# Partial sums of the second product added in DRAM by accumulating transfers, in a two-layer kernel with linear attention ahead of it

## The chip, the cores and the metric

The kernel runs on one core of a Trainium2 chip. A core has a matrix engine (TensorE, PE in the profile, with its weight loads counted apart as PEld), a vector engine (VectorE, DVE), an engine for functions of one operand (ScalarE, ACT), a general one (GpSimd, POOL) and one that here only issues transfers (SyncE, SP). SBUF is the working memory, PSUM holds the sums of the matrix products in banks, and DRAM holds inputs, outputs and buffers. Each engine works through its own list of instructions in order. The metric is the device time of one execution, in microseconds (us); lower is better.

## The reference

Eight batches and eight heads of 576 rows of 64 values are first taken through linear attention and a normalisation; the heads are then laid side by side, so that 4608 tokens of 512 values go through two dense layers with a softplus between them.

```python
kv = einsum('bhsd,bhse->bhde', k, v)
out = einsum('bhsd,bhde->bhse', q, kv)
x = out / sqrt(mean(out * out, -1) + 1e-6) * g_norm   # (8, 8, 576, 64)
x = x.transpose(0, 2, 1, 3).reshape(4608, 512)
h = x @ w_in                                          # w_in  (512, 2048)
g = maximum(h, 0) + log1p(exp(-abs(h)))
result = g @ w_out                                    # w_out (2048, 512)
```

The last line is the second product. The result has 4608 x 512 values of 32 bits.

## The kernel before, in words

**Tiles and phases.** The 4608 tokens are 36 tiles of 128 rows (t), and 12 blocks of three tiles, 384 tokens (n). The 2048 middle columns are 16 chunks of 128 (c). A step is one block with one chunk: the first product gives 128 x 384 values of h in a PSUM bank (mm1, L660, twelve matrix instructions, since each factor is split into three parts that TensorE multiplies and adds up); ScalarE applies the softplus (L683) and rounds off a first part (L685); VectorE makes the second and third part (L672, L676); and the second product adds the chunk's share to three banks of 128 x 512 sums, one for each tile of the block (mm2, L667, nine instructions).

The split weights of 16 chunks don't fit, so the work is cut into three phases (ENDS, L184): in phase 0 the first four blocks take chunks 0 to 3 and the others 0 to 5, in phase 1 chunks 4 to 7 and 6 to 10, in the last phase the rest. That is 64, 56 and 72 steps, in the order phase, block, chunk (ORDER, L243). Phase 0 also does the attention: it builds kv, multiplies by q, normalises (rows, with the root taken on POOL in L528 and L529) and stores the x of later blocks in DRAM. In the other phases x is loaded again (x_again, L638) and split again (L445 on ScalarE, L448 and L452 on VectorE).

**Partial sums between phases.** At the end of a block in a phase the three banks hold partial sums. `leave` (L708) has ScalarE evict each into an SBUF buffer (L711), and SP stores it (L726) in a buffer in DRAM of its own, one for each phase and tile. When the block comes round in the next phase, `enter` (L701) has SP load that buffer (L704) and ScalarE copy it into the bank (L706), and the second product goes on adding to it: its first instruction starts a new sum only in phase 0 (L668). In the last phase the eviction multiplies by a factor (scale, from whole_scale, 1 + 1/4096 unless a weight is out of range) and the store goes to the output.

**Turned tiles.** For tiles 12 to 32 the rows of x were transposed in blocks of 32 x 32 by VectorE, which leaves the tokens of a block in another order. Their results go to the output in four stores of 32 rows each (L718 to L721) instead of one.

**What sets the order.** The program is written in a fixed order by a planner (Plan, L41). Each piece of work is a task with an engine, a cost in ns, the tasks it follows, a position, and the buffers it takes and gives back; a transfer also has a cost for the DMA engines. The planner plays these through and emits each engine's instructions in the order it found. What a task really waits for at run time is set by semaphores. SBUF buffers of 128 x 512 values come from a ring of 13 (m), two more from a ring called x; the second product's banks are the rings s0, s1 and s2, with one bank each, so a block's bank must be evicted before the next block's sums can begin.

```python
def mm2(i):
    if c == cs[0] and ph == 0:
        new(mine[i], [P, d_model])
    for m in range(3):
        nc.tensor.matmul(mine[i].tile, lhsT=gv.tile[:, m, i * P:(i + 1) * P], rhs=w_out.tile[:, m],
                         start=(ph == 0 and c == cs[0] and m == 0), stop=(c == cs[-1] and m == 2),
                         skip_group_check=True)
```

The functions in full, with the line numbers of the profile:

Of the kernel before, what the change touches and what calls it, by code (L numbers as in the profile page):

```python
# [8 lines left out]
F32 = mybir.dt.float32  # L9
# [3 lines left out]
AF = mybir.ActivationFunctionType  # L13
ALU = mybir.AluOpType
# [4 lines left out]
P = 128  # L19
# [4 lines left out]
E = 1.0 / RADIX  # L24
# [16 lines left out]
class Plan:  # L41
# [15 lines left out]
    def slot(self, ring):  # L57
        return Slot(ring)

    def add(self, engine, ns, run, after=(), pos=0.0, take=(), give=(), size=0, behind=None, follows=None):  # L60
        t = Task(engine, ns, run, [a for a in after if a is not None], pos, list(take), list(give), size)
        for s in t.give:
            s.readers += 1
        self.tasks.append(t)
        t.follows = follows
        t.behind = behind
        return t
# [79 lines left out]
def kernel(  # L147
# [24 lines left out]
    nc = tc.nc  # L172
    B, H, S, D = q.shape
    d_model, d_ff = moe_w_in.shape
# [5 lines left out]
    TB = NT // P  # L180
    n_blocks = n_tokens // NT
    n_tiles = n_tokens // P
# [5 lines left out]
    LAST = PHASES[-1]  # L188
# [4 lines left out]
    CONVERT, FETCH, EARLY, LATER = P0[:8], P0[8:16], P0[16:27], P0[27:]  # L193
    BY_PE = 12
# [7 lines left out]
    dram = ctx.enter_context(tc.tile_pool(name="dram", bufs=1, space=DRAM))  # L202
# [10 lines left out]
    scale = const.tile([P, 1], F32, name="scale")  # L213
# [9 lines left out]
    slot, add = plan.slot, plan.add  # L223

    def new(s, shape, dtype=F32):
        if s.ring == "o":
            s.tile = o_banks[:, :, s.place]
            return s.tile
        pool = ps if s.ring in PS else sb
        s.tile = pool.tile(shape, dtype, tag=f"{s.ring}_{s.place}", name=f"{s.ring}_{s.place}")  # L230
        return s.tile
# [21 lines left out]
    factors_done = {}  # L253
# [156 lines left out]
    BL = 32  # L410
# [232 lines left out]
    part = {}  # L643
# [3 lines left out]
    def step(s):  # L647
        ph, n, c = ORDER[s]
        cs = CHUNKS[ph, n]
        h, g, gv = slot("h"), slot("g"), slot("gv")  # L650
        if c == cs[0]:
            sums[:] = [slot(f"s{i}") for i in range(TB)]
        xv, w_in, w_out = xv_slots[ph, n], w_slots[0, c], w_slots[1, c]
        mine = list(sums)

        def mm1():
            hp = new(h, [P, NT])
            for m in range(3 * KD):
                i, kd = divmod(m, KD)
                nc.tensor.matmul(hp, lhsT=w_in.tile[:, i, kd * P:(kd + 1) * P], rhs=xv.tile[:, i, kd],  # L660
                                 start=(m == 0), stop=(m == 3 * KD - 1))

        def mm2(i):
            if c == cs[0] and ph == 0:
                new(mine[i], [P, d_model])
            for m in range(3):
                nc.tensor.matmul(mine[i].tile, lhsT=gv.tile[:, m, i * P:(i + 1) * P], rhs=w_out.tile[:, m],  # L667
                                 start=(ph == 0 and c == cs[0] and m == 0), stop=(c == cs[-1] and m == 2),  # L668
                                 skip_group_check=True)

        def low():
            nc.vector.tensor_tensor(out=gv.tile[:, 1], in0=g.tile, in1=gv.tile.bitcast(F32)[:, 0], op=ALU.subtract)  # L672

        def less():
            f32 = gv.tile.bitcast(F32)
            nc.vector.scalar_tensor_tensor(out=gv.tile[:, 2], in0=f32[:, 1], scalar=-RADIX, in1=f32[:, 0],  # L676
                                           op0=ALU.mult, op1=ALU.add)

        a = mm1s[s] = add("PE", 2100, mm1, x_split[ph, n] + factors_done[0, c] + [mm1s.get(s - 1)] +

                (factors_done[1, ORDER[s - 2][2]] if s > 1 else []), s, [h],
                ([xv] if c == cs[-1] else []) + ([w_in] if s == last_step[c] else []))
        a = add("ACT", 490, lambda: nc.scalar.activation(new(g, [P, NT]), h.tile, func=AF.Softplus, scale=1.0 + E),  # L683
                [a], s, [g], [h])
        a = add("ACT", 530, lambda: nc.scalar.activation(new(gv, [P, 3, NT], F32R)[:, 0], g.tile, func=AF.Copy, scale=DOWN),  # L685
                [a], s, [gv])
        a = add("DVE", 570, low, [a], s, [], [g])
        a = add("DVE", 570, less, [a], s)
        for i in range(TB):
            last = c == cs[-1]  # L690
            seed = [enter(ph, n * TB + i, mine[i], s + 1)] if ph and c == cs[0] else []
            a2 = add("PE", 700, lambda i=i: mm2(i), [a] + factors_done[1, c] + [mm2s.get(i)] + seed, s + 1.5,
                     [mine[i]] if c == cs[0] and not ph else [],
                     [gv] + ([w_out] if s == last_step[c] else []))
            mm2s[i] = a2
            if last:
                leave(ph, n * TB + i, mine[i], a2, s + 1.5)

    sums, mm2s = [], {}

    def enter(ph, t, bank, pos):  # L701

        pt = slot("m")
        ld = add("SP", 350, lambda: nc.sync.dma_start(out=new(pt, [P, d_model]), in_=part[ph - 1, t][0]),  # L704
                 [part[ph - 1, t][1]], pos - EARLY[10], [pt], [], 900, behind=int(pos) - 4)
        return add("ACT", 600, lambda: nc.scalar.copy(new(bank, [P, d_model]), pt.tile), [ld], pos, [bank], [pt])  # L706

    def leave(ph, t, bank, done, pos):  # L708

        ot = slot("m" if ph == 0 else ("m", "x", "m")[t % TB] if ph == LAST else "m")  # L710
        a = add("ACT", 690 if ph == LAST else 600, lambda: nc.scalar.activation(  # L711
            new(ot, [P, d_model]), bank.tile, func=AF.Copy, scale=scale if ph == LAST else 1.0),
            [done] + (scale_done if ph == LAST else []), pos, [ot], [bank])
        if ph == LAST and BY_PE <= t < n_tiles - TB:
            n, i = divmod(t, TB)

            def store():
                for m in range(P // BL):  # L718
                    a, u = divmod(P // BL * i + m, TB)
                    row = n * NT + u * P + a * BL  # L720
                    nc.sync.dma_start(out=out[row:row + BL], in_=ot.tile[m * BL:(m + 1) * BL])  # L721

            part[ph, t] = None, add("SP", 1600, store, [a], pos, [], [ot], 750)
            return
        dst = out[t * P:(t + 1) * P] if ph == LAST else dram.tile([P, d_model], F32, name=f"part{ph}_{t}")
        st = add("SP", 350, lambda: nc.sync.dma_start(out=dst, in_=ot.tile), [a], pos, [], [ot], 720)  # L726
        part[ph, t] = dst, st

    def whole_scale(pos):

# [25 lines left out]
    for c in range(KF):  # L756
        for j in (2 * c, 2 * c + 1):
            pos = CONVERT[j] if c < 4 else LATER[c - 4] + LATER[12] * (j % 2)
# [11 lines left out]
    for s in range(len(ORDER)):  # L770
        if s == first_step[LAST, 0]:
            whole_scale(s - 4)
        step(s)
# [42 lines left out]
```

## Time and profile before

| | |
|---|---|
| median of nine runs | 908.25 us (907.71 to 911.38) |
| the profiled execution, own time | 909.17 us |
| its span, first instruction to last | 907.4 us |
| mean granted clock of TensorE | 0.996 |
| PE busy | 894.7 us |
| ACT busy | 482.7 us |
| of it, copies of partial sums into banks (L706) | 39.2 us, 72 of them |
| POOL busy | 82.7 us |
| transfers: stores of partial sums, loads of them | 72 and 72, of 256 KB |

The profile shows one execution. A row of a group gives line, engine, operation, what it writes and reads, shapes and count, then busy time in us and the mean length of one in ns, and then how long the engine was idle just before, with the line that ended the wait. A row of a transfer gives how many there were, their size, and the median time from the issue to the landing of the data. "SPq" is the list of transfers that SP issues. A share of busy time is a mean over the whole span; phases 1 and 2, in which the partial sums are loaded and copied, run from about 367 us on.

### The profile page before, as it was taken

The page shows a single profiled execution, that of the slowest core. Times are in us where ns is not written, and L with a number is a line of the kernel's source. Part 1 is how long each engine was busy: PE and PEld are TensorE (multiplying, and loading weights), DVE is VectorE, ACT ScalarE, POOL GpSimd, SP SyncE. Part 2 cuts the span into 40 slices and gives each one's busy share as a digit, 9 for nine tenths or more (in the row PEclk, how much of TensorE's full clock was granted, in tenths as well). Part 3 has the DMA queues.
Part 4 walks back from the last instruction along what each step waited for, and adds up shares of the span by engine and source line. Part 5 has one row for each costly group of instructions (what it writes and reads, how often), then busy time and mean ns, then how long its engine had stood idle before and what let it go on. Part 6 is the DMA issues. An engine that isn't in the chain of part 4 may idle for free.

```text
span 907.4 us, 15751 instructions
## 1 busy us (share of the span) xinstructions
PE 894.7 (99%) x5984; PEld 789.5 (87%) x5984; DVE 577.0 (64%) x982; ACT 482.7 (53%) x932; POOL 82.7 (9%) x79
## 2 busy tenths in 40 slices
PE   7999999999999999999999999999999999999998
PEld 5677888888888899999899998989999998999987
DVE  6887888676577877867666667786424444444442
ACT  4776555433444556765656666665433444444453
POOL 0433322122213200000000000000000000000000
PEclk8999999999999999999999999999999999999999
DMA  9999978578672626366344346551330433333322
GB/s 251 258 207 284 248 173 227 133 164 184 185 156 47 164 94 186 105 199 184 105 128 129 128 152 204 186 167 35 105 105 1 140 105 103 107 105 104 105 70 71
DMA packets 211837, 131.60 MB, mean 145 GB/s; under 512 B 102704, under 2 KB 185648, under 8 KB 211760
## 3 DMA queue, kind: packets, MB, share of 16 engines
q1 hardware_dynamic: 211600, 130.59, 52.7%
q8 instruction: 47, 0.77, 0.4%
q14 instruction: 30, 0.25, 0.1%
q10 hardware_dynamic: 160, 0.00, 0.0%
HBM read 91.75 MB, written 38.80 MB: 144 GB/s over the span
## 4 chain that ended last, share of the span: by engine, by line
PE 95%; DMA 3%; ACT 1%; SPq 0%; DVE 0%; issue 0%
PE h L660 44%; PE s L667 44%; DMA m<-in_v_dram 2%; PE o_banks L521 2%; PE tp L502 2%; PE h L780 1%; PE s L502 1%; DMA m<-x 0%; PE tp L577 0%; DVE xv L448 0%; PE tp L539 0%; ACT m L599 0%; ACT xv L445 0%; PE h L374 0%; ACT x L590 0%
## 5 line engine op out<-in xcount | busy, mean ns | idle before, releaser
L660 PE MATMUL h<-xv,w 128*128 128x384 f32 x2304 | 433.8, 337 | 0.2 <-ACT w L378 0.2
L667 PE MATMUL s<-w,gv 128*128 128x512 f32 x1728 | 432.7, 395 | 0.0
L660 PEld LDWEIGHTS h<-xv,w 128*128 128x128 f32 x2304 | 406.3, 188 | 15.7 <-ACT w L378 0.7
L667 PEld LDWEIGHTS s<-w,gv 128*128 128x128 f32 x1728 | 319.7, 188 | 61.3 <-DVE gv L676 0.2
L672 DVE TENSOR_TENSOR gv<-g,gv 128x384 fp32r<-128x384 f32 x192 | 106.6, 555 | 260.3 <-ACT gv L685 259.8
L683 ACT ACTIVATE g<-h 128x384 f32<-128x384 f32 x192 | 94.4, 492 | 321.3 <-PE h L660 314.5
L685 ACT ACTIVATE gv<-g 128x384 fp32r<-128x384 f32 x192 | 100.9, 525 | 36.6 <-PE s L667 25.6
L676 DVE SCALAR_TENSOR_TENSOR gv<-gv 128x384 fp32r<-128x384 f32 x192 | 106.5, 555 | 5.2
L448 DVE SCALAR_TENSOR_TENSOR xv<-m,g_col,xv 128x512 fp32r<-128x512 f32 x102 | 75.9, 744 | 3.3 <-ACT xv L445 3.2
L452 DVE SCALAR_TENSOR_TENSOR xv<-xv 128x512 fp32r<-128x512 f32 x108 | 74.3, 688 | 2.4
L445 ACT ACTIVATE xv<-m,g_down 128x512 fp32r<-128x512 f32 x102 | 69.8, 712 | 0.7 <-DMA m<-x 0.6
L529 POOL TENSOR_TENSOR r<-r,half 128x8 f32<-128x8 f32 x36 | 65.2, 1812 | 3.0
L711 ACT ACTIVATE m<-s 128x512 f32<-128x512 f32 x72 | 39.8, 593 | 4.7 <-PE s L667 2.0
L706 ACT COPY s<-m 128x512 f32<-128x512 f32 x72 | 39.2, 601 | 0.0
L528 POOL TENSOR_SCALAR r<-r 128x8 f32<-128x8 f32 x36 | 16.5, 459 | 219.2 <-DVE r L525 218.7
L533 DVE TENSOR_TENSOR x<-o_banks,r 128x512 f32<-128x512 f32 x36 | 24.8, 688 | 15.0 <-POOL r L529 9.4
L359 DVE TENSOR_TENSOR m<-m,w 128x512 f32<-128x512 f32 x30 | 20.5, 686 | 13.8 <-ACT w L356 10.3
L521 PEld LDWEIGHTS o_banks<-kv,m 64*64 64x64 f32 x1152 | 19.9, 134 | 10.7 <-issue 4.7
L311 ACT ACTIVATE sq<-sq,big 128x512 bf16<-128x512 bf16 x32 | 22.9, 716 | 11.5 <-DVE m L307 11.5
L525 DVE TENSOR_REDUCE r<-x 128x8 f32<-128x512 f32 x36 | 24.3, 679 | 4.8 <-ACT x L590 4.5
L521 PE MATMUL o_banks<-kv,m 64*64 64x64 f32 x1152 | 24.6, 224 | 1.2 <-ACT m L584 0.7
L590 ACT ACTIVATE x<-o_banks 128x512 f32<-128x512 f32 x36 | 21.2, 594 | 7.4 <-PE o_banks L521 3.9
(71 smaller groups left out, 425.0 us busy)
## 6 DMA issues: line engine op xcount, KB each, us to landing
m<-x SPq DMA_DIRECT2D x102, 256.0 KB, 5.0
part<-m SPq DMA_DIRECT2D x72, 256.0 KB, 2.5
m<-part SPq DMA_DIRECT2D x72, 256.0 KB, 4.6
raw<-in_moe_w_in_dram SPq DMA_DIRECT2D x16, 512.0 KB, 5.6
m<-in_k_dram SPq DMA_DIRECT2D x32, 256.0 KB, 5.0
m<-in_v_dram SPq DMA_DIRECT2D x32, 256.0 KB, 4.7
raw<-in_moe_w_out_dram SPq DMA_DIRECT2D x16, 512.0 KB, 5.9
qa<-in_q_dram SPq DMA_DIRECT2D x48, 144.0 KB, 5.0
```

The lines of the kernel that those rows point to most:

```text
L445: nc.scalar.activation(cols(0, F32R), x.tile, func=AF.Identity, scale=g_down)
L448: nc.vector.scalar_tensor_tensor(out=cols(1, F32R), in0=x.tile, scalar=g_col, in1=cols(0), op0=ALU.mult, op1=ALU.subtract)
L452: nc.vector.scalar_tensor_tensor(out=cols(2, F32R), in0=cols(1), scalar=-RADIX, in1=cols(0), op0=ALU.mult, op1=ALU.add)
L521: nc.tensor.matmul(y[r0:r0 + P // 2, a, c0:c0 + D], lhsT=qT.tile[e * D:(e + 1) * D, p, r0:r0 + P // 2], rhs=kvs[b % 2][e * D:(e + 1) * D, ...
L529: nc.gpsimd.tensor_tensor(out=r.tile, in0=r.tile, in1=half, op=ALU.pow)
L660: nc.tensor.matmul(hp, lhsT=w_in.tile[:, i, kd * P:(kd + 1) * P], rhs=xv.tile[:, i, kd], start=(m == 0), stop=(m == 3 * KD - 1))
L667: nc.tensor.matmul(mine[i].tile, lhsT=gv.tile[:, m, i * P:(i + 1) * P], rhs=w_out.tile[:, m], start=(ph == 0 and c == cs[0] and m == 0), s ...
L672: nc.vector.tensor_tensor(out=gv.tile[:, 1], in0=g.tile, in1=gv.tile.bitcast(F32)[:, 0], op=ALU.subtract)
L676: nc.vector.scalar_tensor_tensor(out=gv.tile[:, 2], in0=f32[:, 1], scalar=-RADIX, in1=f32[:, 0], op0=ALU.mult, op1=ALU.add)
L683: a = add("ACT", 490, lambda: nc.scalar.activation(new(g, [P, NT]), h.tile, func=AF.Softplus, scale=1.0 + E), [a], s, [g], [h])
L685: a = add("ACT", 530, lambda: nc.scalar.activation(new(gv, [P, 3, NT], F32R)[:, 0], g.tile, func=AF.Copy, scale=DOWN), [a], s, [gv])
L711: a = add("ACT", 690 if ph == LAST else 600, lambda: nc.scalar.activation(new(ot, [P, d_model]), bank.tile, func=AF.Copy, scale=scale if p ...
```

## The change

Partial sums are no longer brought back. The second product starts a new sum in every phase, each phase's share is evicted as before, and from phase 1 on it is added to what lies in DRAM: POOL issues a transfer that reads the destination and adds the SBUF buffer to it (`accum_op=ALU.add`), after the eviction and after the tile's earlier store or accumulate. There is one place in DRAM for a tile in place of one for each phase. For the tiles that are not turned this place is the output itself, so the last accumulate finishes the result. For the 21 turned tiles it is a buffer; when the last accumulate has landed, SP stores it from DRAM to the output in the four pieces of 32 rows. Since each share is now scaled by itself, the evictions of phases 0 and 1 multiply by 1 + 1/4096 (E is 1/4096) where they multiplied by 1. `enter`, with its loads and copies, is gone. For the planner, the accumulate is a task on POOL of 1100 ns and 900 ns of DMA, and the final copies stand two positions later than the eviction.

```diff
         def mm2(i):
-            if c == cs[0] and ph == 0:
+            if c == cs[0]:
                 new(mine[i], [P, d_model])
             for m in range(3):
                 nc.tensor.matmul(mine[i].tile, lhsT=gv.tile[:, m, i * P:(i + 1) * P], rhs=w_out.tile[:, m],
-                                 start=(ph == 0 and c == cs[0] and m == 0), stop=(c == cs[-1] and m == 2),
-                                 skip_group_check=True)
+                                 start=(c == cs[0] and m == 0), stop=(c == cs[-1] and m == 2))
...
             last = c == cs[-1]
-            seed = [enter(ph, n * TB + i, mine[i], s + 1)] if ph and c == cs[0] else []
-            a2 = add("PE", 700, lambda i=i: mm2(i), [a] + factors_done[1, c] + [mm2s.get(i)] + seed, s + 1.5,
-                     [mine[i]] if c == cs[0] and not ph else [],
+            a2 = add("PE", 700, lambda i=i: mm2(i), [a] + factors_done[1, c] + [mm2s.get(i)], s + 1.5,
+                     [mine[i]] if c == cs[0] else [],
                      [gv] + ([w_out] if s == last_step[c] else []))
...
-    def enter(ph, t, bank, pos):
-
-        pt = slot("m")
-        ld = add("SP", 350, lambda: nc.sync.dma_start(out=new(pt, [P, d_model]), in_=part[ph - 1, t][0]),
-                 [part[ph - 1, t][1]], pos - EARLY[10], [pt], [], 900, behind=int(pos) - 4)
-        return add("ACT", 600, lambda: nc.scalar.copy(new(bank, [P, d_model]), pt.tile), [ld], pos, [bank], [pt])
-
     def leave(ph, t, bank, done, pos):
 
         ot = slot("m" if ph == 0 else ("m", "x", "m")[t % TB] if ph == LAST else "m")
         a = add("ACT", 690 if ph == LAST else 600, lambda: nc.scalar.activation(
-            new(ot, [P, d_model]), bank.tile, func=AF.Copy, scale=scale if ph == LAST else 1.0),
+            new(ot, [P, d_model]), bank.tile, func=AF.Copy, scale=scale if ph == LAST else 1.0 + E),
             [done] + (scale_done if ph == LAST else []), pos, [ot], [bank])
-        if ph == LAST and BY_PE <= t < n_tiles - TB:
+        turned = BY_PE <= t < n_tiles - TB
+        if ph == 0:
+            dst = dram.tile([P, d_model], F32, name=f"part_{t}") if turned else out[t * P:(t + 1) * P]
+            st = add("SP", 350, lambda: nc.sync.dma_start(out=dst, in_=ot.tile), [a], pos, [], [ot], 720)
+        else:
+            dst, st = part[ph - 1, t]
+            st = add("POOL", 1100, lambda: nc.gpsimd.dma_start(out=dst, in_=ot.tile, accum_op=ALU.add), [a, st], pos, [], [ot], 900)
+        part[ph, t] = dst, st
+        if ph == LAST and turned:
             n, i = divmod(t, TB)
 
             def store():
                 for m in range(P // BL):
                     a, u = divmod(P // BL * i + m, TB)
                     row = n * NT + u * P + a * BL
-                    nc.sync.dma_start(out=out[row:row + BL], in_=ot.tile[m * BL:(m + 1) * BL])
-
-            part[ph, t] = None, add("SP", 1600, store, [a], pos, [], [ot], 750)
-            return
-        dst = out[t * P:(t + 1) * P] if ph == LAST else dram.tile([P, d_model], F32, name=f"part{ph}_{t}")
-        st = add("SP", 350, lambda: nc.sync.dma_start(out=dst, in_=ot.tile), [a], pos, [], [ot], 720)
-        part[ph, t] = dst, st
+                    nc.sync.dma_start(out=out[row:row + BL], in_=dst[m * BL:(m + 1) * BL])
+
+            add("SP", 1600, store, [st], pos + 2, [], [], 750)
```

## The prediction, on record before the result

> **What bounds the kernel now.** I read the page first: busy times, the chain that ended last, and the rows of what the change touches.
>
> ```profile
> PE 894.7 (99%) x5984; PEld 789.5 (87%) x5984; DVE 577.0 (64%) x982; ACT 482.7 (53%) x932; POOL 82.7 (9%) x79
> ...
> PE 95%; DMA 3%; ACT 1%; SPq 0%; DVE 0%; issue 0%
> ...
> L529 POOL TENSOR_TENSOR r<-r,half 128x8 f32<-128x8 f32 x36 | 65.2, 1812 | 3.0
> ...
> L706 ACT COPY s<-m 128x512 f32<-128x512 f32 x72 | 39.2, 601 | 0.0
> L528 POOL TENSOR_SCALAR r<-r 128x8 f32<-128x8 f32 x36 | 16.5, 459 | 219.2 <-DVE r L525 218.7
> ...
> part<-m SPq DMA_DIRECT2D x72, 256.0 KB, 2.5
> m<-part SPq DMA_DIRECT2D x72, 256.0 KB, 4.6
> ```
>
> TensorE (PE) is the chain; the work to be removed (the L706 copies, the m<-part loads) is on engines with time to spare. Whether any of it delays PE is answered by the list of waits, for PE alone, whole span: us in total, times, longest.
>
> ```profile
> PE s L502 <- DMA m<-in_v_dram: 4.5, 2, 3.3
> PE h L780 <- DVE ident_r L748: 1.6, 1, 1.6
> PE o_banks L521 <- ACT m L584: 0.7, 3, 0.3
> ...
> PE h L660 <- ACT w L378: 0.2, 1, 0.2
> ```
>
> The eight entries add up to 8.6 us, and none is L667, the product whose banks the L706 copies fill. The first of those copies starts at 370.9 us. So I asked for busy time from there to the end of the matmuls; columns are window, length, then PE, PEld, DVE, ACT, POOL busy (instructions), granted clock, DMA share, GB/s:
>
> ```profile
> 367.00:904.00 537.00, 536.52 (x2694) 485.52 (x2692) 298.75 (x508) 288.43 (x558) 0.00 (x0) 1.00 0.39 119
> ```
>
> PE is busy from edge to edge (its last matmul ends at 903.53), at full granted clock. That is 128 steps; the chain shows one first product every 4.19 us (717.18, 721.36, 725.55), whether a block begins there or not. POOL does nothing here. So nothing removed can shorten this stretch. What remains is the end, from the timeline: start, length, engine, line:
>
> ```profile
> 902.17 0.69 ACT L711 ACTIVATE m<-s,scale 128x512 f32<-128x512 f32 x1 [1.77 <-PE s L667]
> 902.87 0.69 ACT L711 ACTIVATE x<-s,scale 128x512 f32<-128x512 f32 x1
> 902.88 0.35 SPq L726 DMA_DIRECT2D out_dram<-m  x1
> 903.56 0.69 ACT L711 ACTIVATE m<-s,scale 128x512 f32<-128x512 f32 x1
> 903.58 0.35 SPq L726 DMA_DIRECT2D out_dram<-x  x1
> 904.27 0.33 SPq L726 DMA_DIRECT2D out_dram<-m  x1
> ```
>
> Three evictions, three stores. The row of this line from 610 us on gives 2.0/2.1/2.7 us (min/median/max) from issue to landing, so the last store lands at 904.27 + 2.1 = 906.37, and the span ends 1.03 us later, at 907.4.
>
> **What the change does to each part.** *Removed:* 72 loads of 256 KB and 72 ScalarE copies of 601 ns (43 us by count, 39 us of busy time). At block ends the first product's bank was evicted, copied into and then read: in the last such place the third eviction ends at 885.38, the three copies run 885.27 to 886.90, and L667 resumes at 886.59 without idle time. Without the copies the bank is ready earlier, and PE still comes out of a 12-matmul first product (884.48 to 886.75) that nothing shortens. Gain: 0. What is late next is PE itself.
>
> *Changed, same cost:* evictions get another constant factor (588 ns stays). Phase 0's stores go to out or a part buffer, same queue and size. PE's list of instructions has the same 971 rows; from the end of phase 0 on, a few first products stand one place earlier or later, at no cost while PE has no idle time.
>
> *Moved, in the middle:* the 36 stores of phase 1 and 15 of the last phase become accumulating transfers on POOL, and the 21 turned tiles get one more each: 72 in order on POOL. POOL's last arithmetic (L529) starts at 310.9 us and phase 1's first evictions at 385.57, so none delays the roots of phase 0. Each waits for its eviction and for the tile's earlier store or accumulate, which is a whole phase old (over 200 us); behind a waiting one stand only other accumulates. Three per block take 3 x 1.13 us (below) of the 17 us of four steps: hidden. An eviction waits for the accumulate that last read its buffer; with two x buffers that is two blocks back, 42 us.
>
> The 21 turned tiles still end as 84 stores on SP, now from DRAM to DRAM, and SP waits for each tile's accumulate first; the x loads for the block three later stand behind. In the old trace block 8's first eviction ends at 842.35, its twelve stores run from 842.38 to 847.9, three m<-part loads to 849.6, the x loads issue from 849.70, and ScalarE reads them from 866.85. After: the first accumulate lands at 842.38 + 1.13 + 2.95 = 846.5 (values below), twelve stores take 5.4 us to 851.9, loads issue to 853.5 and land in 5.3 (their median): 858.8, 8 us early. With the high ends the third accumulate lands at 842.38 + 5.43 + 4.14 = 851.95, its stores end at 853.8, and the loads land by 861. Cost 0; what exceeds the 8 us would hold ScalarE, with the next activation queued behind, once per block. Block 10's own copies come 42 us after block 8's, at worst landing 4.6 us (a load's median) after 895.8: 900.4, before the new end.
>
> DMA: 18.9 MB of loads go, the accumulates read as much, and the turned stores add 5.5 MB of reads; the DMA share there is 0.39. Cost 0.
>
> *Moved, on the path:* the last three stores. No transfer issued by POOL is in this trace, so two unknowns are bounded. Issue time d on POOL: the nearest rows are its own, 459 ns for a small operation and 1812 ns for the one it computes longest; the mean, 1.13 us, is my value (the planner's own entry for it, 1100, is close). Flight f after issue: at least the store's, 2.1 - 0.33 = 1.77 us; at most that plus a whole load before it, since the destination must be read: the quickest m<-part load lands in 2.7 us, 2.37 after issue, so 4.14. I take the middle, 2.95, because reading and writing share parts of both. Neither unknown can be below its bound enough to gain: the evictions end at 904.25 either way, and the third cannot issue before.
>
> The first issues at 902.88, the third at 902.88 + 2 x 1.13 = 905.14 (later than its eviction, so POOL's queue decides), ends 906.27, lands 909.22; plus 1.03 the span ends at 910.25. That is **+2.85 us**. With both low ends: third issue 904.27, landing 904.27 + 0.46 + 1.77 = 906.50, +0.1. With both high ends: 902.88 + 5.43 + 4.14 = 912.45, +6.1.
>
> The profiled execution took 909.17 us with a span of 907.4; the sum makes it 912.0. The median of nine runs is 908.25, 0.9 lower; there the sum gives 911.1.
>
> Two rules of the Trainium skill speak against this change. The trace has a 256 KB store landing in 2.1 us from SP. "DMA: Bandwidth & Descriptors", section "Latency and other measured facts", puts the first byte of a GpSimd-issued transfer at about 1 us against 0.6; by that alone the end would move by about 0.4 us, an estimate that leaves out queueing and the read. The trace has L672 at 548 ns mean between 60 and 300 us, where POOL is active, and 559 between 660 and 900, where it is not: no sign that the two disturb each other. "SBUF — State Buffer", in its box on VectorE blocking DMA, says a two-port VectorE copy locks GpSimd out of writing descriptors; by it accumulates in phase 1, beside L298 and L315, would be late. The last L315 starts at 610.6, so the end would be untouched; no run here shows the rule.
>
> **Rivals.** *Not slower: the accumulate costs what a store does.* Place: the last three transfers. Speaking for it: 64 KB and 256 KB stores land in 1.7 and 2.1 us, so the data itself is cheap, and a POOL row of 237 ns exists (L528's shortest). Price: +0.1 us with both low ends, 908.4. It decides from +1.8 us (0.2%, about what a measurement of this kernel can tell from no change) downward: the last landing must come before 906.37 + 1.8 = 908.17, so with d = 0.46 (third issue ending at 904.73) f must stay under 3.44 us, with d = 1.13 (906.27) under 1.9. Against: it needs both unknowns low, and the addition has to read.
>
> *Much slower: the middle gives way.* Either POOL's issues hold up VectorE, or accumulates move slowly. In a leaving step VectorE ends the operand at 884.83 and PE's weight load reads it at 886.42, a margin of 1.59 us; three holds of 1.13 would pass it by 1.8 us, and 23 blocks would pay 41 us: 952. The even 548/559 ns above speak against it. Slow transfers: 192 KB more cost a store 0.4 us, so 256 KB move in about 0.55 us; at ten times that the last three take 16 us in a row, 904.0 + 16.5 + 1.77 + 1.03 = 923.3, +16: 924. Nothing in the trace suggests such a factor.
>
> *Faster.* If the removed 43 us of ScalarE work had held PE back. PE's waits after 367 us are 0.0 to two digits; the 0.48 us left over in the window lies after its last matmul. The most it could give is nothing; I leave a small chance for what the trace cannot show, 906.
>
> *That the change doesn't do what it says:* instruction lists show 72 transfers added on POOL and the 72 loads and copies gone; what could be missing is only the gain, which is the forecast.
>
> **Chances.** Slower by the tail alone, +1.8 to +6.1: 0.70. As cheap as a store: 0.18. The middle gives way, or a tail beyond 6.1: 0.09. Faster: 0.03. So faster 0.03, within 0.2% 0.18, slower 0.79. The range: from 908.8 (into the cheap case) to 914.3 (high ends, 908.25 + 6.1); left out are about 0.08 below and 0.09 above.
>
> **What would show it.** Right: PE without idle time from 367 us to its last matmul at 903.5; three POOL transfers at the end, the third starting later than its eviction's end at 904.25; the last landing near 909.2. ScalarE's busy time down by about 39 us, the span no shorter. Wrong: PE waits at L667 or L660 in phases 1 and 2 (the middle), a POOL issue near SP's 0.33 us with a landing near 2 us (rival one), or a last landing after 912.5.

## The result, and the profile after

The changed kernel takes 916.1 us (median of 9 runs, 915.49 to 917.51), against 908.98 for the kernel before (29 runs): a ratio of 1.008, 95% interval 1.007 to 1.0089. The profiled execution took 915.49 us with a span of 913.7, 6.3 more than before. Slower was forecast, but by 2.85 us, and 916.1 lies above the range's high end of 914.3.

The page after the change (the q0 row is a transfer queue: packets, MB, share of the 16 transfer engines' span):

```profile
span 913.7 us, 15603 instructions
...
PE 894.2 (98%) x5984; PEld 789.0 (86%) x5984; DVE 581.0 (64%) x982; ACT 449.1 (49%) x860; POOL 147.3 (16%) x151
...
q0 software_dynamic: 10368, 18.88, 14.1%
...
L711 POOL DMA_DIRECT2D part<-m x35 | 35.1, 1193 | 255.7 <-ACT m L702 236.7
...
part<-m POOLq DMA_DIRECT2D x35, 256.0 KB, 6.2
```

PE does the same work in the same time, ScalarE is 33.6 us less busy (about 39 were forecast), and POOL issues 72 transfers, about 1.2 us each, through a queue of its own. That queue holds the transfer engines for 14.1% of 913.7 us, which is 1.79 us of all sixteen for each accumulate. Phases 1 and 2, by windows (window, length, then PE, PEld, DVE, ACT, POOL busy):

```profile
367.00:903.00 536.00, 536.00 (x2691) 485.01 (x2690) 302.22 (x508) 253.35 (x485) 61.38 (x70) 1.00 0.44 95
```

PE is busy from edge to edge, as before; its last matmul ends at 903.20 (903.53 before). So the middle neither gained nor lost, and all of the loss comes after it. The end, by the timeline (evictions are now L702, the accumulates L711):

```profile
901.84 0.69 ACT L702 ACTIVATE m<-s,scale 128x512 f32<-128x512 f32 x1 [1.77 <-PE s L667]
902.54 0.69 ACT L702 ACTIVATE x<-s,scale 128x512 f32<-128x512 f32 x1
902.82 0.86 POOL L711 DMA_DIRECT2D out_dram<-m  x1 [15.99 <-ACT m L702]
903.23 0.69 ACT L702 ACTIVATE m<-s,scale 128x512 f32<-128x512 f32 x1
903.52 1.05 POOL L711 DMA_DIRECT2D out_dram<-x  x1
904.21 1.25 POOL L711 DMA_DIRECT2D out_dram<-m  x1
```

The three issues overlap: each starts 0.29 us after its eviction, though each takes about 1 us. How long they fly is a row of the output tensor, for this window; the second row is the same for the kernel before:

```profile
DMA to landing us min/median/max: 3.6/5.2/5.7
```

```profile
DMA to landing us min/median/max: 2.0/2.0/2.1
```

The last accumulate lands at 909.95 (904.21 + 5.74), the last store of before landed at 906.31. And then the end of the program does not follow. Instructions of the closing barrier, after and before (count, then ns min/median/max, first and last start):

```profile
L806 POOLq DRAIN  x3: 40/102/8745, 904.2 to 913.4; - x3
L806 SPq DRAIN  x3: 7/7/136, 910.9 to 913.2; - x3
```

```profile
L811 POOLq DRAIN  x3: 40/82/2054, 310.8 to 907.1; - x3
```

After the change POOL's first closing drain, the instruction that waits until all its work is done, starts at 904.19 and takes 8745 ns. It ends at 912.94, 2.99 us after the last landing, while SP has seen every landing, has drained too, and has waited since 911.06. Before, POOL's drain was over by 313 us.

From the end of the last eviction to the end of the span it is now 9.80 us (903.92 to 913.72) instead of 3.14 (904.25 to 907.39), 6.66 more, in three terms: eviction to third issue 0.03 to 0.29, **+0.27**; issue to landing 2.04 to 5.74, **+3.70**; landing to end 1.08 to 3.77, **+2.69**. PE being 0.33 us earlier in this execution makes it the 6.3 of the spans. The last term is the drain's 2.99 and 0.78 of closing steps behind it; before, SP was through 0.38 us after the last landing and the steps behind it took 0.70.

The medians lie 7.1 us apart, more than these spans. The third accumulate's flight varies: in five other kernels below that end with three whole ones it is 6.2 to 6.8 us, so the 5.7 here is at the short end. That this makes up the rest of the difference fits its size, but is not shown.

### The profile page after: what moved, and what is told of

It is laid out like the page before. It is cut to its first block, busy times and chain, and to the rows that moved or that the text cites. A ratio compares the mean times of both kernels' runs of the same rounds, so it can differ in the third digit from the quotient of the medians.

```text
span 913.7 us, 15603 instructions
## 1 busy us (share of the span) xinstructions
PE 894.2 (98%) x5984; PEld 789.0 (86%) x5984; DVE 581.0 (64%) x982; ACT 449.1 (49%) x860; POOL 147.3 (16%) x151
## 3 DMA queue, kind: packets, MB, share of 16 engines
q0 software_dynamic: 10368, 18.88, 14.1%
HBM read 78.38 MB, written 44.30 MB: 134 GB/s over the span
## 4 chain that ended last, share of the span: by engine, by line
issue 58%; PE 28%; POOL 7%; DMA 3%; DVE 1%; ACT 1%; SPq 0%; POOLq 0%
PE h L660 11%; PE s L667 11%; POOL part L711 4%; POOL out_dram L711 3%; DMA m<-in_v_dram 2%; PE o_banks L521 2%; PE tp L502 2%; PE h L775 1%; PE s L502 1%; DMA raw<-in_moe_w_in_dram 1%; DVE xv L448 0%; PE tp L577 0%; ACT m L599 0%; PE o_banks L539 0%; PE tp L539 0%
## 5 line engine op out<-in xcount | busy, mean ns | idle before, releaser
L671 DVE TENSOR_TENSOR gv<-g,gv 128x384 fp32r<-128x384 f32 x192 | 106.7, 556 | 242.9 <-ACT gv L684 242.2
L711 POOL DMA_DIRECT2D part<-m x35 | 35.1, 1193 | 255.7 <-ACT m L702 236.7
L711 POOL DMA_DIRECT2D out_dram<-m x25 | 25.1, 1192 | 273.6 <-ACT m L702 273.6
L702 ACT ACTIVATE m<-s 128x512 f32<-128x512 f32 x72 | 39.9, 592 | 4.7 <-PE s L667 2.0
```

What stands on the lines that cost most here:

```text
L711: st = add("POOL", 1100, lambda: nc.gpsimd.dma_start(out=dst, in_=ot.tile, accum_op=ALU.add), [a, st], pos, [], [ot], 900)
```

## The experiments

The theory after this reading: the middle costs nothing; the accumulates hold the transfer engines longer, so that the last three queue; and POOL's drain runs on after the last landing. The rivals: the loss comes with any use of these transfers, each accumulate has a long flight of its own, or the drain's length has another cause. Four kernels first.

**Block 11 of the last phase as before the change, the other 69 accumulates kept.**

```diff
+    def old(ph, t):
+        return ph == LAST and t in (n_tiles - 3, n_tiles - 2, n_tiles - 1)
...
+            seed = [enter(ph, n * TB + i, mine[i], s + 1)] if old(ph, n * TB + i) and c == cs[0] else []
...
+        elif old(ph, t):
+            dst = out[t * P:(t + 1) * P]
+            st = add("SP", 350, lambda: nc.sync.dma_start(out=dst, in_=ot.tile), [a], pos, [], [ot], 720)
```

> The changed kernel, but block 11 in the last phase as before the change: its three partial sums are loaded and copied into the banks (by a ScalarE activation that divides by 1 + 1/4096), and SP stores its results. The other 69 accumulates stay. Theory: the whole loss lies in the last three transfers and in POOL's closing drain behind them, the middle costs nothing. Then the span is 907.4 +- 0.7 us and the time within 0.15% of the kernel before; POOL's drain ends long before SP's last store lands. Rival: the loss, or the 2.7 us of it after the last landing, comes with any use of accumulating transfers from POOL; then 2.5 us or more remain and the span is 910 us or more.

Measured: ratio 1.0002 (0.999 to 1.0014), the time of the kernel before. The profiled span is 908.9, a little over the expected band; in that execution PE ends about 0.9 us later, and from the last eviction to the end it is 3.73 us, its last store having landed after 2.6 us instead of 2.0. Its windows and its drain:

```profile
367.00:904.00 537.00, 537.00 (x2697) 486.26 (x2697) 303.56 (x510) 255.16 (x488) 61.28 (x69) 1.00 0.44 97
```

```profile
L823 POOLq DRAIN  x3: 40/102/9297, 886.6 to 908.6; - x3
```

69 accumulates beside the matmuls cost nothing, and neither does the drain when it runs from 886.57 to 895.87, beside block 11's steps. It also shows what the removal is worth: 69 of 72 loads and copies are gone and the time is the same.

**Block 11's stores from POOL, without addition, in the kernel before.**

```diff
+        if ph == LAST and t >= n_tiles - TB:
+            st = add("POOL", 1100, lambda: nc.gpsimd.dma_start(out=dst, in_=ot.tile), [a], pos, [], [ot], 900)
```

> The kernel before, with block 11's last three stores issued by POOL without addition. Theory A (addition slows the packets, and the drain follows the last landing): packets of 85 ns as from SP, last landing about 907 us, a drain that ends some 3 us after it, span 910.5 to 911.2. Theory B (the drain has a fixed length of 8.7 us after the last issue): span 913.5. Theory C (drain and long flight both belong to the addition): span 908 to 908.5.

Measured: ratio 1.0004 (0.9994 to 1.0014), span 908.4. This is theory C. Its landings and drain:

```profile
DMA to landing us min/median/max: 2.6/2.7/2.8
```

```profile
L814 POOLq DRAIN  x3: 40/93/2952, 904.5 to 908.1; - x3
```

A plain transfer from POOL flies 0.6 to 0.7 us longer than one from SP. From the last eviction to the end it is 4.17 us, 1.03 more than before, which the ratio's interval is too wide to show. The drain ends at 907.41, 0.17 us after the landing: neither 3 us behind it nor of fixed length. That it belonged to the addition was the natural reading, and wrong, as the later runs show. The section "Anatomy of one DMA" of the Trainium skill's "DMA: Bandwidth & Descriptors" gives 2.0 us + bytes / 436e3 for a transfer issued by GpSimd; for 256 KB that is an estimate of 2.6 us, which these rows bear out (39 plain transfers below: 2.3 to 2.7 at the end).

**One accumulate left at the end** (`old` without the last tile).

> As the first, but tile 35 alone, the last, is accumulated by POOL; tiles 33 and 34 are loaded, copied and stored by SP. Theory (the three queue on the DMA engines at 1.4 to 1.8 us each): alone it lands 3.6 us after its issue as the first of three did, at about 907.9, and the span is 911.6. Rival (each accumulate has a long flight of its own): 5.7 us, landing 909.9, span 913.7.

Measured: ratio 1.005 (1.0033 to 1.0067), span 911.9. The one accumulate is the row's maximum, the two others are SP's stores:

```profile
DMA to landing us min/median/max: 2.0/2.1/4.0
```

4.0 us, between the 3.6 and the 5.7: a flight of its own of 1.3 us more than a plain transfer from POOL, and 1.7 us more for the third in a queue. So the theory holds for the queue, while a lone accumulate is dearer than the first of three was. The transfer records of the changed kernel show the queue itself: its last three accumulates hold the engines one after the other, until 906.14, 908.22 and 909.63, and the third, issued at 904.21, moves its first row at 907.90. In this trace's records a row of 2 KB takes an engine 178 ns (median) with the addition and 85 ns without, each engine has eight rows of a transfer, and the slowest row takes 771 ns. The drain again ends 2.91 us after the landing.

**Only block 11's last share accumulated, all else as before the change.**

```diff
+    def fresh(ph, n):
+        return ph == LAST and n == n_blocks - 1
...
+            part[ph, t] = None, add("POOL", 1100, lambda: nc.gpsimd.dma_start(out=dst, in_=ot.tile, accum_op=ALU.add),
+                                    [a, st], pos, [], [ot], 900)
```

> The kernel before, with block 11's last share alone accumulated: its partial sums of phase 1 are stored in the output, scaled by 1 + 1/4096, and three accumulates from POOL end the kernel; all else is loaded and copied. Theory (all of the loss is at the end, and does not depend on how many accumulates there were): span 913.4 to 914, +0.7% as the changed kernel has. Rival (part of it grows with the number of accumulates, the drain above all): less, 911 to 912.5.

Measured: ratio 1.0043 (1.0029 to 1.0058): about half of the loss, the rival's side. The span of 913.2 in the profiled execution misleads, since PE ended 1.4 us later there; from the last eviction to the end it is 7.84 us, 1.96 less than in the changed kernel, although its third accumulate flies longer (6.4 us). The drain:

```profile
L820 POOLq DRAIN  x3: 40/93/6617, 905.6 to 912.9; - x3
```

It ends at 912.24, 0.17 us after the last landing (912.07). Three accumulates and three plain transfers give the same 0.17; 70 and 72 give 2.9 and 3.0. So the drain's tail goes with how many there were, or with something else that changes with it: a longer list of instructions on POOL, whose fetch could stall. Three kernels tell these apart: the last one above with the share of blocks 8 to 11 or of all blocks accumulated (`n >= 8`, `n >= 0`), and with 140 idle instructions on POOL.

> The kernel before, with the last phase's shares of blocks 8 to 11 accumulated (12 transfers from POOL in all, 9 of them by tiles that then go to the output by DRAM to DRAM stores). So far the drain ended 0.17 us after the last landing with 3 transfers from POOL in the kernel and 2.9 to 3.0 us after it with 70 or 72. Theory of a threshold or a step between: at 12 either 0.2 or 2.9 us. Theory of a cost for each: 0.17 + 9 x 0.041 = 0.5 us.

> The same with all 12 blocks of the last phase accumulated: 36 transfers from POOL, phase 1 by loads and copies as before. Theory of a cost for each transfer: the drain ends 0.17 + 33 x 0.041 = 1.5 us after the last landing, span 912.4 plus or minus 1 for the start. Theory of a step: 0.2 or 2.9 us, span 911 or 913.7.

```diff
+        if s == first_step[1, 0] + 4:
+            for _ in range(140):
+                add("POOL", 100, lambda: nc.gpsimd.memset(dummy, 0.0), [mm1s[s]], s)
```

> Only block 11's last share accumulated (3 transfers), with 140 memsets of 128 x 1 values on POOL after the last root, so that POOL's list is as long as the changed kernel's (about 240 instructions) without its transfers. Theory that the late drain comes with the length of POOL's list (an instruction fetch stands near the end of the changed kernel's trace): the drain ends 2.9 us after the last landing. Theory that it comes with the number of transfers: 0.2 us.

And, for the addition against the mere transfer, 39 plain ones (the 36 stores of phase 1 and the last three, `if ph == 1 or ph == LAST and t >= n_tiles - TB`):

> The kernel before, with the 36 stores of phase 1 and the last three issued by POOL without addition: 39 plain transfers from POOL. If the drain's cost belongs to transfers issued by POOL, whatever they do: it ends 0.05 + 39 x 0.041 = 1.65 us after the last landing, span 908.4 + 1.5 = 909.9 (plus or minus 1). If it belongs to the addition: 0.2 us, span 908.4.

The first closing drains of POOL with 140 memsets, with 36 accumulates and with 39 plain transfers (the longest of three in each row):

```profile
L835 POOLq DRAIN  x3: 40/102/6980, 903.3 to 911.0; - x3
L831 POOLq DRAIN  x3: 40/102/7706, 904.0 to 912.2; - x3
L814 POOLq DRAIN  x3: 40/102/4347, 903.6 to 908.5; - x3
```

Measured, with the runs above, all from the traces (us):

| transfers from POOL | last landing | drain ends | after it | 0.05 + 0.041 x count |
|---|---|---|---|---|
| 3 plain | 907.24 | 907.41 | 0.17 | 0.17 |
| 3 accumulates | 912.07 | 912.24 | 0.17 | 0.17 |
| 3 accumulates, 140 memsets | 910.11 | 910.28 | 0.17 | 0.17 |
| 12 accumulates | 910.93 | 911.46 | 0.53 | 0.54 |
| 36 accumulates | 910.16 | 911.68 | 1.52 | 1.53 |
| 39 plain | 906.34 | 907.98 | 1.64 | 1.65 |
| 70 accumulates | 908.18 | 911.09 | 2.91 | 2.92 |
| 72 accumulates (the changed kernel) | 909.95 | 912.94 | 2.99 | 3.00 |

The drain takes 41 ns for each transfer that POOL has issued, with addition or without, and the length of POOL's list has no part in it: with 140 memsets it has 241 instructions, against 239 in the changed kernel. The spans of the four were 912.2, 912.5, 911.2 and 908.8 us; each is a single execution, so they carry about 1 us of the start's scatter.

**A drain of POOL placed earlier in the changed kernel.**

```diff
+        if ph == LAST and t == n_tiles - TB - 1:
+            add("POOL", 9000, lambda: nc.gpsimd.drain(), [st], pos + 0.1)
```

> The changed kernel, with one drain of POOL added behind block 10's last accumulate, so that it runs beside the matmuls of block 11. Theory (the closing drain takes 41 ns for each transfer that POOL issued since its last drain): the added drain ends 0.05 + 69 x 0.041 = 2.9 us after its landing, near 896 us, the closing one 0.17 us after the last landing; span 913.7 - 2.8 = 910.9 (plus or minus 1 for the start), time +0.45% on the kernel before. Rival (the count runs from the start of the kernel, or a drain costs what it costs whenever it comes): the closing drain still ends 2.9 us or more after the last landing, span 913.7, +0.8%.

Measured: ratio 1.006 (1.0047 to 1.0073), span 911.8. The added drain and the closing one:

```profile
L714 POOLq DRAIN  x1: 9861/9861/9861, 884.5 to 884.5; - x1
```

```profile
L808 POOLq DRAIN  x3: 46/102/6744, 903.4 to 911.5; - x3
```

The added one ends at 894.35, 2.86 us after its landing (891.49), beside the matmuls. The closing one ends at 910.10, 0.16 us after the landing at 909.94. So the count starts again at a drain: the theory. The ratio is above the 1.0045 that was expected, and its interval just meets that of the changed kernel (1.007 to 1.0089). The expectation went by the changed kernel's profile; the third accumulate flew 6.6 us here, 0.8 more than there.

Of the 2.69 us between landing and end that the changed kernel lost, 0.78 stays (1.87 us against 1.08). With POOL's drain out of the way SP is the last. Its drains in this kernel and in the kernel before:

```profile
L808 SPq DRAIN  x3: 7/7/135, 910.8 to 911.3; - x3
L811 SPq DRAIN  x3: 7/7/7, 906.6 to 906.9; - x3
```

At the end SP looks at the transfer semaphores, two with each instruction, 0.06 us apart. It has eight of POOL's as well, four instructions more behind the last landing (0.29 us); then it pauses for 0.34 us where there were 0.04, and its first drain takes 135 ns instead of 7. What the pause waits for no run shows. In the changed kernel all this is hidden, since SP is through at 911.06 and POOL's drain ends at 912.94.

**Each of the last three accumulates in two halves of 1 KB rows.**

```diff
+                W = d_model // 2
+                st = add("POOL", 1100, lambda: put(slice(0, W)), [a, st], pos, [], [ot], 900)
+                st = add("POOL", 1100, lambda: put(slice(W, 2 * W)), [st], pos, [], [ot], 900)
```

> The changed kernel, with each of block 11's last three accumulates as two of 128 x 256 (rows of 1 KB instead of 2), first halves of all three ahead of the second halves. In the changed kernel a row of 2 KB took 178 ns with the addition, 85 ns without. If the addition costs by the byte, a row of 1 KB takes about 90 ns and the last landing comes at about the same time (6 us after the last eviction, plus three more issues of about 1 us): span 914 to 916. If it costs by the row, 178 ns, the transfers take 3 x 1.4 us longer: span 918.

Measured: a single execution, 916.8 us, span 915.1. A row of 1 KB takes 102 ns, so the addition is paid mostly by the byte. The last landing comes 7.32 us after the last eviction instead of 6.03: smaller pieces are no way out. The drain ends 3.11 us after the last landing; POOL has issued 75 transfers, six of them halves, and 0.05 + 0.041 x 75 is 3.13, so a half costs the drain as much as a whole.

No run beats the kernel before; the first matches it, as PE without idle time in the middle leaves nothing to gain there.

## Why the prediction was wrong, point by point

- **"Nothing removed can shorten this stretch": right.** PE is busy for all of 536 us, and with 69 of 72 copies and loads gone the ratio is 1.0002. The share of the transfer engines there rose from 0.39 to 0.44, at no cost, as forecast.
- **Turned stores and x loads, cost 0: right, with the times off.** The x loads for block 11 were to issue from 851.9; they issue from 854.81, since the twelve DRAM to DRAM stores ahead of them start at 847.04, not 846.5, and take SP 7.67 us (587 ns each by the median) where 5.4 was taken. ScalarE reads the loads from 864.01, not 866.85. PE did not wait.
- **POOL's issues hold up VectorE: no.** The second operand's row (now L671) has a mean of 559 ns between 660 and 900 us, as before.
- **The three issues in a row at 1.13 us each, the third at 905.14: wrong by size.** The lengths were about right (0.86, 1.05, 1.25), but they overlap, so the third starts at 904.21. The term was 0.6 us too dear, counted from the last eviction.
- **The flight after issue, 2.95 us between 1.77 and 4.14: wrong, outside the bounds.** From the end of the third issue (905.47) to landing it is 4.48. The upper bound put one quiet load ahead of one quiet store and let three transfers fly side by side. An accumulate holds the transfer engines twice as long as a store (178 ns for each row against 85), so the third waits for the two before it. Of the +3.70 from issue to landing, about 0.7 is what a plain transfer from POOL flies longer, 1.3 the addition and 1.7 this queue. The prediction had such a queue only in its rival at ten times a store's duration, not at twice.
- **"The span ends 1.03 us later" than the last landing: the step that failed.** It was carried over from SP's stores as a constant. With POOL's transfers it is 3.77 us, 2.7 more: POOL's drain ends 0.05 us + 41 ns for each of its 72 transfers behind the landing, and the closing steps follow it. This alone puts the time outside the range. The landing came 0.73 us later than predicted (909.95 for 909.22, with PE 0.33 earlier) and was within its bounds, since the errors of issue and flight partly cancel, which is luck; without the 2.7 us behind it the median would be 913.4, below the range's end of 914.3.
- **The rivals.** An accumulate as cheap as a store: no, 178 against 85 ns for each row. The middle giving way: no. What came true was the other half of that case, "a tail beyond 6.1".
- **The two rules of the Trainium skill.** The later first byte, an estimate of 0.4 us, has the sign of the 0.3 to 0.7 us by which plain transfers from POOL fly longer, a small part of the loss. VectorE locking out POOL's descriptors: every run ended with VectorE idle, so no run shows it at the end. In phase 1 of the changed kernel an L298 (404.62 to 405.04) ran beside the accumulate issued at 404.57, which took 1.55 us; one issued at 638.45, with VectorE idle, took 1.49. So the rule's delay was not seen there either.

One more page bears on the addition. The records have 178 against 85 ns for each 2 KB row, 2.1 times. "Collectives: The Full Stack", section "The bandwidth ceiling: the fold count and why AG ≠ RS ≠ AR", says that a reduce-scatter in the transfer engines is slower than an all-gather because its addition reads two sources, with a measured ratio of 1.93. The sizes agree. That the read of the destination is the second source here is not shown: the profile's HBM reads fall from 91.75 to 78.38 MB, by the 18.9 of the loads less the 5.5 of the turned stores, so it does not count such a read.

## What to carry to other kernels

Work that moves from an engine with time to spare to the transfer queues gains nothing while the matrix engine is busy from edge to edge, and what it costs shows where nothing covers it, at the end of the program. Keep transfers issued by POOL, accumulating ones above all, out of the last few microseconds: in the middle 69 of them were free. If they must stand there, put a drain of POOL ahead of them while the matrix engine works: POOL's closing drain then ended 0.16 us after the last landing instead of 2.99, and the ratio went from 1.008 to 1.006.

## What the runs showed of the hardware

A drain of POOL ends 0.05 us + 41 ns for each transfer issued from POOL since its last drain after the last of them has landed (0.17 us at 3, 1.52 at 36, 1.64 at 39 plain ones, 2.99 at 72). Why a drain has a price for each transfer stays open; no run here looks inside it. Issues from POOL of about 1 us each overlap, one starting every 0.7 us as evictions allow. An accumulate of 128 rows of 2 KB holds the sixteen engines for 1.79 us (14.1% of the span for 72), a plain transfer from POOL for 0.75 (39 take 3.2% of 908.8 us):

```profile
q0 software_dynamic: 3120, 10.23, 3.2%
```
